# A linear-attention and long-convolution kernel with a new written-out order, the last inverse transform folded, and four output buffers

## The chip, the cores and the metric

The kernel runs on one core of a Trainium2 chip. The metric is the device time of one launch in microseconds: the median of three runs, and beside it one execution taken by the hardware profiler. The engines are named as the profile names them: PE (TensorE), DVE (VectorE), ACT (ScalarE), POOL (GpSimd), and SP, whose queue issues nearly all transfers.

## The reference, cut to what matters

Two layers, one behind the other, for 4 batches of 768 steps, 8 heads of 48 (together 384 channels):

```python
# 1: a recurrence over the steps, for each batch and head; state is 48 x 48
for t in range(S):
    cur   = einsum('bhd,bhe->bhde', u[None] * kt, vt)         # the "bonus"
    y[t]  = einsum('bhd,bhde->bhe', rt, state + cur)
    state = wt[..., None] * state + einsum('bhd,bhe->bhde', kt, vt)
# 2: x = y as (4, 768, 384)
x1, x2, x3 = split(x @ w_proj)                                # 384 -> 3 x 384
conv = irfft(rfft(x2, axis=1) * rfft(filter_fft, axis=0), axis=1)
out  = (x1 * conv * x3) @ w_out
```

## The kernel before, in words

**Chunks.** The steps are cut into chunks of 128, six to a batch, 24 in all; the number behind an operation's name is the chunk (`kq23`). Loads come in groups: chunks 0, 1, then 2 and 3, 4 and 5, and so on in pairs. For a chunk, `lw`, `lk`, `lr`, `lv` are its four loads of 192 KB (SP, L1313). `ln` takes the logarithm of w (ACT), `cs` sums it along the chunk (PE), `ex` takes the exponential in PSUM (ACT, L1353), `kq` multiplies it with k and r (DVE, L1356), `tr` and `qk` transpose that, `sc` is the product of scores in PSUM, `mt` copies it out under the causal mask: on DVE the mask is multiplied in (L1396), on ACT it is a plain copy and POOL cuts it afterwards (`mc`, L1401); either takes one half (letters D, A, G) or both halves at once (M, N, C). `kv`, `ki` and `su` carry the state on; `yi`, `ys`, `y` make the chunk's output in PSUM, `xn` copies it (or adds the bonus term on the way, letter V), `xa` adds the bonus on POOL after a copy to f32 (letter X), `yt` and `xT` transpose it for the second layer. The bonus term is `rk` (r times k), `ru` (the bonus product, times u), `rh` (halves added), `cc` (summed), `vc` (times v).

**Batches.** Names with two or three numbers belong to the second layer, the first number being the batch. `p` and `q` are the projections x1 and x3 (PE), `cp` copies x1 out, `cq` multiplies x3 in PSUM with it: the gate (DVE, L1649). `xw` and `cxw` make x2, `sd` adds and subtracts its two halves of the sequence, `f` is the forward transform as a matrix product, `cf` its copy, `u0`, `u1` and `p` followed by the batch and one more number (`p3.2`) the complex product with the filter's spectrum (DVE, L1695 to L1698), `E` the inverse transform for one block of 128 channels. Its copy `cE` (ACT) and two instructions `aE` on DVE (L1738, L1742) put the even and the odd part together. Where the inverse is folded (letter Q) PE multiplies fewer columns, 2 of 384 and 4 of 192 rather than 6 of 384, and `aE` leaves two interleaved halves in a second buffer, which the pair `dE` (L1751) adds and subtracts. `yE` multiplies with the gate, `o` is the last projection, `co` copies it out of PSUM to an output buffer, `so` stores that (SP, L1796). Batch 3 does this in smaller pieces: `sd`, `u` and `p` in thirds, `E3` in three parts for each block (`E3.2`, `E3.2.0`, `E3.2.2`), `o` in parts by block.

**Order.** Nothing is scheduled when the kernel runs. `ORDER` (L43 to L1068) lists all operations; each line has the name, the engine's letter, for PE the first PSUM bank, and at times the name of a DVE operation behind which this one is to start (a tie that keeps POOL and DVE apart, L1848). A `-` leaves an optional operation out. Each engine takes its operations strictly in that order and waits by semaphores. `warm n b` puts n filler matmuls on PE. Buffers are rings: three for w, four for k and r and for v, three for `xn`, and `NO` = 5 for the output; the ring's places are given in the order in which the stores are defined (batch 0: 0, 1, 2; batch 1: 3, 4, 0; batch 2: 1, 2, 3; batch 3: 4, 0, 1, 2). The last inverse, `E3`, is not folded; its six products `yE3` are on DVE but for `yE3.0.1` and `yE3.1.1`, which are POOL's.

Of the kernel before, what the change touches and what calls it, by code (L numbers as in the profile page):

```python
# [38 lines left out]
NLW, NLD, NG, NF, NS, NX, NO = 3, 4, 3, 4, 3, 3, 5  # L39
# [6 lines left out]
pads D  # L46
smalls D
zeros D
lw0 S
first A  # L50
ln0 A
imaps G
maske G smalls
maps G smalls
ang2 D
ang1 D
lw3 S
lw2 S
lr0 S
lk0 S  # L60
kz2 G
maskn G
cs0 P 4
kz0 G
ln2 A
u S
signs D
maski G
ia1.0 G
ex0 A  # L70
kq0 D
ia2.0 D
warm 9 1
cs3 P 6
kz3 G zeros
cs2 P 2
ur A
warm 5 1
um P 0
rk0 G  # L80
ub A
lv0 S
lw1 S
lr3 S
lk1 S
tr0 P 1
qk0 D
ph0 A
vb0 A
ex3 A  # L90
ln1 A
ang0 D
ru0 G ia2.0
rh0 G kq0
cc0 D
kz1 D
vc0 D
warm 6 0
sc0 P 0
warm 2 4  # L100
cs1 P 4
mt0.1 -
mt0.0 N
kv0 P 0
ex2 A
ex1 A
ia0.0 G zeros
su0 D
mc0.0 C cc0
lk3 S  # L110
lr1 S
mc0.1 -
warm 4 1
yi0 P 0
kq3 D
y0 P
xn0 A
tr3 P 1
kq1 D
lk2 S  # L120
lr2 S
lv1 S
lw4 S
lw5 S
tr1 P 0
rk1 G
ru1 D
rh1 G ru1
ph1 A
qk3 D  # L130
xa0 -
ph3 A
kq2 D
lv2 S
lv3 S
yt0 P 6
sc3 P 4
xT0 A
mt3.0 M
qk1 A  # L140
vb1 A
ph2 A
warm 4 7
tr2 P 6
lr4 S
lk4 S
ki1 P 1
sc1 P 2
qk2 A
mc3.0 -  # L150
mt1.1 -
kv1 P
warm 2 7
sc2 P 6
cc1 D
rk2 G
lk5 S
ru2 D
ia2.1 G
vc1 G  # L160
mc1.1 -
mt1.0 M
mc1.0 -
mt2.1 -
mt3.1 -
lr5 S
ln3 A
warm 5 0
cs4 P 4
yi1 P 2  # L170
rh2 G ru2
su1 D
vb2 G ru2
ys1 P
mc2.1 -
lv5 S
lv4 S
cc2 D
vc2 G cc2
mt2.0 M  # L180
wproj1 G mt2.0
ki2 P 0
y1 P
lw6 S
warm 5 1
kv2 P
xn1 A
ex4 A
cs5 P 2
xa1 -  # L190
mc2.0 -
yt1 P 1
su2 D
ki3 P 0
kv3 P
yi2 P 6
ys2 P
y2 P
mc3.1 -
xT1 A  # L200
kq4 D
# [259 lines left out]
ex11 A
p1.2.0 P 0
# [1416 lines left out]
```

## Time and profile before

| | |
|---|---|
| median of three runs | 157.35 us (157.31 to 157.82) |
| the profiled execution | 153.79 us, span 152.1 us |
| granted clock of TensorE | 1.0 throughout |
| busy: PE, DVE, ACT, POOL | 94%, 89%, 81%, 63% of the span |
| DMA | 26.23 MB; the last load issued at 108.2 us |

The profiled execution is 3.6 us shorter than the median of the runs; all times by stage are from the profiled one. Its rows give an instruction's mean duration in ns, or its start and duration in us; consecutive instructions of DVE overlap a little, so the busy time of a stretch is less than the sum of durations. `kq5` starts at 24.32 us, `kq7` at 35.55, `kq23` at 112.30 (it ends at 113.24); `p3.2`, DVE's last sum ahead of the last inverse, ends at 140.80, and DVE's last `yE3` at 146.17.

### The profile page before, as it was taken

How to read it: one execution, taken by the hardware profiler on the slowest of the kernel's cores; microseconds unless marked ns; L12 is line 12 of the kernel's file. 1: busy time of each engine (PE TensorE's matmuls, PEld its weight loads, DVE VectorE, ACT ScalarE, POOL GpSimd, SP SyncE). 2: the span in 40 equal slices, each digit the busy share in tenths (PEclk: the TensorE clock that was granted, in tenths of full speed). 3: DMA queues.
4: the chain of work that ended last, by engine and by line, in shares of the span. 5: the costliest groups of instructions: out<-in, count | busy, mean ns of one | idle time of the engine just before them, and what ended most of it. 6: DMA issues, size and time to landing. Idle time of an engine off the chain costs nothing.

```text
span 152.1 us, 4409 instructions
## 1 busy us (share of the span) xinstructions
PE 142.4 (94%) x1725; PEld 95.3 (63%) x1725; DVE 135.6 (89%) x252; ACT 123.1 (81%) x204; POOL 96.1 (63%) x101
## 2 busy tenths in 40 slices
PE   7986999999999999999999999999999999999980
PEld 5654667666556657567666776576687666656530
DVE  3589996989969999999989999999999999999950
ACT  4576849989979989997889899979999987576370
POOL 6577989944069567888968974885299164830310
PEclk9999999999999999999999999999999999999999
DMA  4999899999999999989899899998940000002956
GB/s 97 216 214 223 163 221 174 203 182 272 250 209 170 197 172 219 212 162 218 170 203 218 160 203 192 198 213 169 324 133 0 4 0 0 4 0 88 395 210 240
DMA packets 104118, 26.23 MB, mean 172 GB/s; under 512 B 100129, under 2 KB 102690, under 8 KB 104098
## 3 DMA queue, kind: packets, MB, share of 16 engines
q1 hardware_dynamic: 102498, 24.78, 74.2%
q0 software_dynamic: 1600, 1.18, 5.6%
q8 instruction: 13, 0.21, 0.5%
q14 instruction: 7, 0.06, 0.1%
HBM read 22.41 MB, written 4.72 MB: 178 GB/s over the span
## 4 chain that ended last, share of the span: by engine, by line
PE 42%; DVE 15%; DMA 13%; SPq 10%; ACT 8%; issue 5%; POOL 4%; POOLq 1%; DVEq 0%; ACTq 0%
SPq L1313 10%; PE banks L1624 7%; PE banks L1511 6%; PE banks L1780 5%; DMA w<-in_w_dram 5%; PE banks L1661 3%; PE banks L1368 3%; PE banks L1380 3%; DMA v<-in_v_dram 3%; DMA kr<-in_r_dram 3%; DVE kq L1356 3%; PE banks L1458 3%; DMA kr<-in_k_dram 2%; ACT banks L1353 2%; PE banks L1716 2%
## 5 line engine op out<-in xcount | busy, mean ns | idle before, releaser
L1209 POOL TENSOR_TENSOR rk<-kr 128x768 bf16<-128x768 f32 (+1 forms) x13 | 23.0, 1766 | 9.5 <-DMA kr<-in_r_dram 5.9
L1624 PE MATMUL banks<-xT,wproj 128*128 128x384 bf16 x144 | 27.9, 326 | 0.2 <-ACT x L1213 0.2
L1356 DVE TENSOR_TENSOR kq<-banks,kr 128x768 bf16<-128x768 f32 x24 | 22.4, 949 | 3.6 <-DMA kr<-in_k_dram 1.7
L1401 POOL TENSOR_SCALAR_AFFINE_SELECT mt<-mt 128x512 bf16<-128x512 bf16 (+1 forms) x15 | 14.0, 940 | 12.7 <-ACT mt L1213 8.6
L1209 POOL TENSOR_TENSOR vc<-vb,cc 128x768 bf16<-128x768 bf16 (+1 forms) x11 | 17.4, 1577 | 5.1 <-DVE cc L1332 3.3
L1353 ACT ACTIVATE banks<-banks 128x768 f32<-128x768 f32 x24 | 19.1, 806 | 0.5 <-PE banks L1350 0.2
L1624 PEld LDWEIGHTS <-wproj 128*128 128x128 bf16 x144 | 13.0, 97 | 8.1 <-issue 0.7
L1213 ACT ACTIVATE x<-banks 128x768 bf16<-128x768 f32 (+1 forms) x24 | 16.8, 709 | 1.6 <-PE banks L1661 1.1
L1396 DVE TENSOR_TENSOR mt<-banks,mask_excl 128x1024 bf16<-128x1024 f32 (+1 forms) x17 | 16.2, 965 | 0.2 <-PE banks L1380 0.2
L1213 ACT ACTIVATE qk<-banks 128x1024 bf16<-128x1024 bf16 x16 | 16.2, 1029 | 0.0
L1368 PE MATMUL banks<-ident,kq 128*128 128x128 bf16 x192 | 14.3, 219 | 1.4 <-ACT xn L1213 0.6
L1259 PE MATMUL banks<-wt 128*128 128x256 bf16 x90 | 14.4, 300 | 1.1 <-DVE wt L1282 1.1
L1368 PEld LDWEIGHTS <-kq 128*128 128x128 bf16 x192 | 11.8, 97 | 4.2 <-DVE kq L1356 1.6
L1780 PE MATMUL banks<-wout,y 128*128 128x384 bf16 x72 | 13.3, 326 | 0.5 <-DVE g L1649 0.3
L1661 PE MATMUL banks<-wproj,xT 128*128 128x384 bf16 x72 | 13.6, 325 | 0.0
L1511 PE MATMUL banks<-sd,F 128*128 128x384 bf16 (+1 forms) x96 | 13.4, 328 | 0.2 <-ACT phi L1360 0.2
L1319 ACT ACTIVATE lg<-w 128x768 bf16<-128x768 f32 (+1 forms) x13 | 10.4, 799 | 3.4 <-DMA w<-in_w_dram 3.4
L1213 ACT ACTIVATE mt<-banks 128x512 bf16<-128x512 f32 (+1 forms) x15 | 11.6, 802 | 1.1 <-PE banks L1380 0.7
L1213 ACT ACTIVATE o<-banks 128x768 f32<-128x768 f32 (+1 forms) x12 | 9.3, 785 | 3.5 <-PE banks L1780 3.4
L1511 PEld LDWEIGHTS <-F 128*128 128x128 bf16 (+1 forms) x120 | 8.5, 103 | 5.8 <-issue 1.1
L1649 DVE TENSOR_TENSOR g<-banks,x 128x384 bf16<-128x384 f32 (+1 forms) x16 | 11.8, 748 | 0.3 <-PE banks L1624 0.2
L1209 DVE TENSOR_TENSOR U<-X,hh 128x2304 bf16<-128x2304 bf16 (+1 forms) x12 | 11.9, 1022 | 0.0
(109 smaller groups left out, 331.1 us busy)
## 6 DMA issues: line engine op xcount, KB each, us to landing
w<-in_w_dram SPq DMA_DIRECT2D x24, 192.0 KB, 4.4
kr<-in_r_dram SPq DMA_DIRECT2D x24, 192.0 KB, 3.9
kr<-in_k_dram SPq DMA_DIRECT2D x24, 192.0 KB, 3.8
v<-in_v_dram SPq DMA_DIRECT2D x24, 192.0 KB, 3.9
out_dram<-o SPq DMA_DIRECT2D x11, 384.0 KB, 4.0
U<-in_moe_filter_fft_dram SPq DMA_DIRECT2D x1, 1152.0 KB, 7.3
wproj<-in_moe_w_proj_dram POOLq DMA_DIRECT2D x3, 288.0 KB, 5.9
out_dram<-o SPq DMA_DIRECT2D x2, 192.0 KB, 2.2
```

Of the source, the lines that this page charges most:

```text
L1209: return eng(e).tensor_mul(o, a, b)
L1213: return nc.scalar.activation(out=o, in_=a, func=AF.Copy)
L1259: nc.tensor.matmul(banks[:, at, 0:256], wt[:, 0:L], wt, start=True, stop=True)
L1313: op(f"l{name}{i}", [SP], lambda e, bk, t=t, x=x, q=q, rw=rw: nc.sync.dma_start(out=t[:, q], in_=x[b, :, rw, :].rearrange("h t d -> t h d" ...
L1353: op(f"ex{i}", [ACT], lambda e, bk: nc.scalar.activation(out=two(bk, f"cs{i}")[:, :, 0:C], in_=two(bk, f"cs{i}")[:, :, 0:C], func=AF.Exp), ...
L1356: op(f"kq{i}", [DVE], lambda e, bk: nc.vector.tensor_mul(kq[f][:, :, :, 0:D], two(bk, f"cs{i}")[:, :, 0:C].rearrange("p a (h d) -> p a h d ...
L1368: nc.tensor.transpose(p[:, HP * m + j, :], kq[f][:, m, 2 * j:2 * j + 2, :], ident)
L1396: return copy(ACT, o, x) if e in (ACT, ACT2) else nc.vector.tensor_mul(o, x, _mid(mask_excl, z - HP * a))
L1511: nc.tensor.matmul(p[rows], F[:, ti, c0 + rows.start:c0 + rows.stop], x[q][:, ti, :], start=(ti == 0), stop=(ti == NT - 1),)
L1624: nc.tensor.matmul(p, wproj[:, cb, col0:col0 + L], xT[bx][:, cb, sl], start=(cb == 0), stop=(cb == CB - 1),)
L1661: nc.tensor.matmul(view(bk)[:, z], xT[bx][:, cb, (c0 + z) * L:(c0 + z + 1) * L], wproj[:, cb, C:2 * C], start=(cb == 0), stop=(cb == CB - 1),)
L1780: nc.tensor.matmul(view(bk)[:, z], yt_[:, z, :], wout[:, cb, :], start=(cb == 0), stop=(cb == CB - 1),)
```

## The change

The order is written anew. It keeps the first layer's loops, the loads and the matrix products; what is moved is the place of nearly every operation in the first 30 us, of fewer behind that, and on which engine the movable ones run. `NO` goes from 5 to 4, so the ring's places are now 0, 1, 2 (batch 0), 3, 0, 1 (batch 1), 2, 3, 0 (batch 2), 1, 2, 3, 0 (batch 3). `xf`, the f32 buffer of the X way, goes from three places to one.

Four optional ways are added to the code. Of these the new order uses: the last inverse folded (all three blocks, with `dE3.2.1` and `dE3.0.1` on POOL and the other four `dE3` on DVE, and all six `yE3` on DVE), and the gate by way of an f32 buffer `xe` for `q0.2.1` and `q3.0.1` (`xq`, a copy on ACT; `gq`, the product on POOL). It doesn't use: the exponential to `xe` with the product on POOL (`ew`, `kw`) and `aE` on POOL (`aw`); all of these are listed with `-`. The bonus product's figure for DVE stands in no file of the kernel; nine of thirteen `ru` are on DVE before and after (`ru0` for `ru9`).

DVE's list ends so (before, after):

```diff
-p3.1 D   -p3.0 D   -p3.2 D   -cq3.2.1 D   -cq3.0.1 D
-aE3.0.1 D   -aE3.0.0 D   -aE3.1.1 D   -aE3.1.0 D   -aE3.2.0 D   -aE3.2.1 D
-yE3.2.1 D   -yE3.2.0 D   -yE3.0.0 D   -yE3.1.0 D   -co3.1 D
+yE2.0 D   +p3.1 D   +u03.2 D   +u13.2 D   +p3.0 D   +p3.2 D   +cq3.2.1 D   +cq3.2.0 D
+aE3.2.0 D   +aE3.2.1 D   +aE3.0.1 D   +aE3.0.0 D   +aE3.1.0 D   +aE3.1.1 D
+dE3.1.1 D   +yE3.0.1 D   +yE3.1.1 D   +yE3.2.1 D
+dE3.0.0 D   +dE3.1.0 D   +yE3.0.0 D   +dE3.2.0 D   +yE3.1.0 D   +yE3.2.0 D
```

POOL's, ACT's and SP's:

```diff
-rk12 G sd2.1.0   -mc20.0 G cq2.0.1   -vc11 G   -xa19 G   -dE1.2.1 G cc11   -dE1.0.1 G
-dE1.0.0 G aE1.1.0   -mc22.0 G yE1.1   -mc22.1 G   -mc23.0 C   -sd3.0.0 G sd3.1.0
-sd3.1.1 G   -sd3.1.2 G sd3.0.2   -dE2.0.0 G aE2.0.1   -dE2.1.1 G   -yE3.0.1 G aE3.0.0   -yE3.1.1 G
+mc20.0 G   +vc11 G   +rk12 G kq22   +dE1.0.1 G aE1.2.0   +xa18 G   +dE1.2.1 G   +rh12 G yE1.1
+mc22.0 C   +sd3.0.1 G sd3.1.2   +sd3.1.1 G sd3.1.2   +dE2.0.1 G   +dE2.0.0 G
+gq3.0.1 G p3.2   +dE3.2.1 G   +dE3.0.1 G aE3.0.0
...
-co2.0 A   -co2.1 A   -cE3.0 A   -cE3.1 A   -cE3.2 A   -co2.2 A   -co3.2 A   -co3.3 A   -co3.0 A
+xq3.0.1 X   +cf3.2 A   +cp3.2.1 A   +co2.2 A   +cE3.2 A   +cE3.0 A   +cE3.1 A   +co2.1 A   +co2.0 A
+co3.3 A   +co3.2 A   +co3.0 A   +co3.1 A
...
-lr23 S   -so0.1 S   -lk23 S   -so0.0 S   -so0.2 S   -lv22 S   -so2.0 S   -so1.1 S   -so1.2 S
-so1.0 S   -so2.1 S   -so2.2 S   -so3.2 S   -so3.3 S   -so3.0 S   -so3.1 S
+lr23 S   +lk23 S   +lk22 S   +so0.0 S   +lr22 S   +lv23 S   +so1.1 S   +so0.1 S   +so1.2 S
+so1.0 S   +so2.2 S   +so0.2 S   +so2.1 S   +so2.0 S   +so3.3 S   +so3.2 S   +so3.0 S   +so3.1 S
```

Further back, DVE loses and gains these (before `-`, after `+`):

```
 to kq5:         -ang2 -mt1.0:M -qk3 -kz1   +ur +ang2 (behind kq4) +qk1 +qk2 +ru0 +rh0 +rh2 +kz3 +ia1.0
 kq5 to kq7:     -cp0.2.0 -cxw0.0 -rh3 -xn3   +if0 +if1 +if3 +mt4.0 +mt4.1 +xT4 +xn2
 kq7 to kq23:    -cq0.2.1 -mt8.0:M -qk13 -qk15 -mt15.0 -mt15.1 -xT13 -cp2.2.1 -mt19.0:M -rh9 -rh10 -ru9
                 +mt8.0 +mt8.1 +xT10 +mt15.0:M +rh8 +xn14:V +yE0.1 +mt19.0 +qk18 +xT16 +xT17 +xn19:V
 kq23 to p3.2:   -rh12 -cq3.2.0 -sd3.0.1 -dE2.0.1   +dE1.0.0 +mt23.0:M +sd3.0.0 +sd3.1.2 +dE2.1.1
```

In the head SP's loads begin `lw0 lw3 lw2 lk0 lr0 u lk1 lr1 lw1 lr3 lk3 lv0` (before: `lw0 lw3 lw2 lr0 lk0 u lv0 lw1 lr3 lk1 lk3 lr1`), the copy `ur` moves from ACT to DVE ahead of `kq0`, and the fillers on PE go from 90 to 98. On PE behind the head the order is nearly the same; `yi18` goes out.

The code:

```diff
-NLW, NLD, NG, NF, NS, NX, NO = 3, 4, 3, 4, 3, 3, 5
+NLW, NLD, NG, NF, NS, NX, NO = 3, 4, 3, 4, 3, 3, 4
+NE = 2
...
+    xe = tiles(NE, [L, 2, H, D], FP32, "xe")
...
-    xf = sb.tile([L, NX, C], FP32, name="xf")
+    xf = sb.tile([L, 1, C], FP32, name="xf")
...
+            op("x" + n3, [WIDE, NONE], lambda e, bk: copy(ACT, x3, view(bk, n3)), w=["x" + n3], uses=[n3], cost=n)
+            op("g" + n3, [POOL, NONE], lambda e, bk: nc.gpsimd.tensor_mul(g[bx][:, fs, sl], x3, x1[:, fs, sl]),
...
-                    op(n if m == 1 else f"{n}.{m}", [PE], part(m, m == 1, m == 2),
+                    op(n if m == 1 else f"{n}.{m}", [PE, FOLD], part(m, m == 1, m == 2),
...
+            half = vl[cb].rearrange("p q h d -> p (q h d)").bitcast(BF16)[:, 0:S].rearrange("p (a t) -> p a t", a=2)
+
+            def other(bk):
+                return half if last else y2[1 - bx][cb]
...
-            if not last:
-                for z in (0, 1):
-                    op(f"d{n}.{z}", [DVE, POOL, NONE], lambda e, bk, z=z: eng(e).tensor_tensor(
-                        out=y[cb][:, z], in0=y2[1 - bx][cb][:, 0], in1=y2[1 - bx][cb][:, 1],
+            for z in (0, 1):
+                op(f"d{n}.{z}", [DVE, POOL, NONE], lambda e, bk, z=z: eng(e).tensor_tensor(
+                    out=y[cb][:, z], in0=other(bk)[:, 0], in1=other(bk)[:, 1],
...
```

## The prediction

> **What bounds the kernel now.** I read the page's busy sums and DMA row first, then a table of stretches, then VectorE's waits, then the groups by shape, and last the order of time around two places.
>
> ```profile
> PE 142.4 (94%) x1725; PEld 95.3 (63%) x1725; DVE 135.6 (89%) x252; ACT 123.1 (81%) x204; POOL 96.1 (63%) x101
> DMA  4999899999999999989899899998940000002956
> ```
>
> ```profile
> 24.30:60.00 35.70, 35.01 (x449) 23.29 (x446) 33.14 (x52) 32.76 (x50) 22.22 (x18) 1.00 1.04 204
> 60.00:113.20 53.20, 52.43 (x704) 35.94 (x702) 51.76 (x85) 48.44 (x84) 39.78 (x34) 1.00 0.98 202
> 113.20:146.20 33.00, 32.81 (x318) 20.76 (x316) 32.71 (x65) 24.37 (x41) 15.31 (x15) 1.00 0.16 61
> ```
>
> In the stretches the columns are PE, weight load, DVE, ACT, POOL. Between 24.3 us (the start of `kq5`) and 146.2 us (the end of the last product on the outputs) DVE is idle for 2.56 + 1.44 + 0.29 = 4.3 us of 121.9. PE looks as full, but its ends are modelled; `mt`, `qk`, `xn` and all else that it needs comes from DVE or ACT. The last loads land at about 114 us, so the 38 us behind them have no transfer to wait for.
>
> ```profile
> DVE kq L1356 <- DMA kr<-in_r_dram: 1.3, 1, 1.3
> DVE hh L1586 <- ACT hh L1585: 0.9, 1, 0.9
> ```
>
> These are the longest waits of DVE in that time; all others are 0.5 us or less. So from 24.3 us on, the end is set by the sum of DVE's work, and I make the sum of that.
>
> ```profile
> L1356 DVE TENSOR_TENSOR kq<-banks,kr 128x768 bf16<-128x768 f32 x24 | 22.4, 949 | 3.6 <-DMA kr<-in_k_dram 1.7 <-DMA kr<-in_r_dram 1.3 <-ACT banks L1353 0.4
> L1396 DVE TENSOR_TENSOR mt<-banks,mask_excl 128x1024 bf16<-128x1024 f32 x9 | 10.9, 1216 | 0.2 <-PE banks L1380 0.2
> L1396 DVE TENSOR_TENSOR mt<-banks,mask_excl 128x512 bf16<-128x512 f32 x8 | 5.3, 682 | 0.0
> L1751 POOL TENSOR_TENSOR y<-y 128x384 bf16<-128x384 bf16 x5 | 4.8, 986 | 0.5 <-DVE y L1738 0.4
> L1751 DVE TENSOR_TENSOR y<-y 128x384 bf16<-128x384 bf16 x7 | 2.1, 352 | 0.0
> ```
>
> ```profile
> 91.46 1.82 DVE L1356 TENSOR_TENSOR kq<-banks,kr 128x768 bf16<-128x768 f32 x2
> ...
> 122.92 2.24 DVE L1209 TENSOR_TENSOR U<-X,hh 128x2304 bf16<-128x2304 bf16 x1
> 120.97 2.99 POOL L1401 TENSOR_SCALAR_AFFINE_SELECT mt<-mt 128x512 bf16<-128x512 bf16 x3 [3.31 <-DVE y L1209]
> ```
>
> Two `kq` of 949 ns take 1.82 us together, so each instruction on a full DVE costs its duration less 0.08 us. The last two lines show the other cost: `u02.0` takes 2.24 us, the other five of its kind 1.34 (9.0 less 2.24, by 5); POOL's masks end at 123.96, and 1.20 us later it is done. It stood behind POOL.
>
> **The change, part by part (DVE, from `kq5` on).**
>
> Head (to `kq5`). `lv0` goes from sixth load to eleventh; by the landings of those places (8.3 and 12.7 us) `vb0`, `kv0` and then `su0` (12.3 us now) move to about 14.5, and DVE queues `vc0`, `cc1` and `kq2` behind `su0`. `ur` (0.5 us on ACT) now stands ahead of `kq0`; `ang2`, two `qk` and `ru0`, `rh0`, `rh2` come in, `mt1.0`, `qk3`, `kz1` go out. DVE is idle for 24.3 − 17.4 = 6.9 us here, and `kq5` waits for the last of the same 23 or 24 loads in both orders (24.2 us). I take 0, with 1 us against it if that cover is short. SP's loads otherwise change places within a few; two of the three stores among the last ones move behind them (about 1 us each: `so0.0` lands at 111.2, `so0.2` at 112.1), but `kq22` then waits for the load next to last, as `kq23` does now: 0. The eight more fillers on PE stand in front of waits: 0, at most 8 × 0.13 = 1 us (six took 0.76 in the chain), under the same cover.
>
> `kq5` to `kq7`. In: `mt4.0`, `mt4.1` (2 × 0.682), `xT4` (0.349), three flips. The trace has no flip on DVE; `dE` (0.352, both operands in SBUF) and the scaled copy `hg` from PSUM (0.552) bound it, and `dE` is nearer: 3 × 0.35. Out: `cxw0.0` (0.949), `cp0.2.0` (0.553), `rh3` (0.364). That is +0.90 for three more instructions: +0.65 us.
>
> `kq7` to `kq23`. In: `mt8` in two halves for one whole (+0.15), `xT10`, `xT16`, `xT17` (1.05), `xn14`, `xn19` (1.10), `yE0.1` (0.55), `rh8` (0.36), `qk18` (0.68). Out: `cq0.2.1` (0.55), `qk13`, `qk15` (1.37), `mt15` halves to a whole (0.15), `xT13` (0.35), `cp2.2.1` (0.55), one half of `mt19` (0.53), `rh9`, `rh10` (0.73), `ru9` (0.63). Sum −0.97 us with as many instructions. The copies and masks that go to ACT fall on an engine idle for 4.8 us of 53 there.
>
> `kq23` to `p3.2`. In: `mt23` (1.216, now on ACT), `dE1.0.0` and `dE2.1.1` (0.35 each), two pieces of `sd3` (0.43 each). Out: `rh12` (0.36), `dE2.0.1` (0.35), one `sd3` (0.43), and `cq3.2.0` (0.55) moves behind `p3.2`. +1.08, one more: +1.0 us.
>
> `p3.2` to the last `yE3`. The last inverse is folded: four `dE3` come to DVE (1.41), two `yE3` come from POOL (0.71), `cq3.2.0` comes here (0.55); `cq3.0.1` goes (0.95) to an ACT copy (0.81) and a POOL product. +1.72, six more: +1.23 us. The POOL product has no row; 0.91 (the 128x384 sum `xn<-xf,vc`) and 1.9 (the 128x768 f32 `rk`) bound it, and `rk` is nearer in size. It starts behind `p3.2`, the first `dE3` on POOL can start 2.2 us later, so it is hidden.
> A folded inverse's six matmuls take 0.66 us in the chain, six of 384 columns 0.97, so PE saves 3 × 0.31 = 0.9 us in E3, but DVE gets little of it: today E3's first copy ends 1.2 us behind `p3.2` and two gates (1.33) hide that; the gates that are left take 0.95, so 0.2 us opens.
>
> The end. Today 5.9 us lie between the last `yE3` on DVE (146.17) and the end:
>
> ```profile
> 143.23 0.85 POOL y L1209
> 144.15 0.95 POOLq L1874
> 145.15 1.16 PE banks L1780 x6
> 146.44 0.81 ACT o L1213
> 147.26 0.59 issue
> 147.85 0.56 DVE o L1215
> ```
>
> PE stands behind POOL's two products until 145.15. With them on DVE, after the last `yE3`: matmuls 0.6, `co3.0` 0.8, `co3.1` on ACT 0.4, then as now 3.7 from the last copy to the end: 5.5. −0.4 us.
>
> Four output buffers. `co1.1` to `co3.1` now wait for another store. The stores of batch 1 are long out; `so0.2`, now behind `so2.2` on SP, lands about 4 us behind `p3.2`, when ACT comes to `co2.0`. `so2.1` and `so2.0` are issued about 4 and 5 us behind `p3.2`; with the 2.3 us of a late store (145.35 to 147.69) they land at 6.3 and 7.4; `co3.2` and `co3.1` want their buffers at 6.5 and 8.3. I take 0; with today's longest late store (4.3) each would be 1 to 2 us late. Below zero: nothing, a buffer less frees nothing sooner.
>
> Clashes with POOL. `u02.0` loses 0.9 us now; the `mc23` it met is gone, since `mt23` masks on DVE. `ru9` (1.22 against 0.55) leaves DVE. New: `dE3.1.1` meets POOL's `dE3.0.1` (0.3), `dE1.2.0` meets `dE1.2.1` (0.3), and what I can't see in a new order, 0 to 2.4 (as much as now). Net I take −0.5, ends −1.5 and +1.5.
> The Trainium skill, page SBUF — State Buffer, section Who interferes with whom, has VectorE with two SBUF inputs and a GpSimd instruction that reads SBUF exclude each other, whichever starts first; by that rule every `dE`, `yE`, `u`, `p`, `ru` on DVE is exposed and `aE`, `kq`, `cq` (one operand in PSUM) aren't. The trace agrees: `u02.0` above ended 1.2 us behind POOL, and the two `kq` beside POOL's `rk10` kept 949 ns.
>
> Sum: 0 + 0.65 − 0.97 + 1.0 + 1.23 + 0.2 − 0.4 − 0.5 = +1.2; a little of the 4.3 us of idle time will close, −0.2. I forecast +1.0 us: the profiled execution from 153.8 (span 152.1) to 154.8; it lies 3.6 us below the median of the runs, 157.35, to which I add the same: 158.3.
>
> **The rivals.**
> Faster: the stalls close. For it: 4.3 us idle and 2.4 us of clashes on DVE between 24.3 and 146.2 us, which another order needn't have. Against it: six of the ten rows of DVE's waits there are 0.4 us or less. The sum without idle and clashes is +1.7 (the terms above less −0.5); it turns when more than 1.7 us of the 6.7 is won. Both large clashes (1.5) and half of the idle time (2) gone: 157.35 + 1.7 − 3.5 = 155.6.
> No change: DVE is not the pace. For it: the chain that ended last is 42% PE, and PE is as full; PE's own work falls by 1.2 us (E3; the `yi` of chunk 18, 0.26). Then DVE's 1.7 us and PE's saving about cancel: 157.3.
> Stores: `co3.2` and `co3.1` wait for `so2.1` and `so2.0`, 1 us on top: 159.3. For it: four late stores took 3 to 4.3 us when issued together; against it: single ones took 1.9 to 2.6.
> Clashes grow: three meetings of 0.67 to 0.9 more, 2 us on top: 160.3. For it: six `dE` and two `yE` with both operands in SBUF come into the last 30 us on DVE; against it: POOL's work after `rk12` falls by 2.9 us.
>
> **How the numbers follow.** Forecast 0.42, stalls close 0.30, no change 0.13, stores 0.08, clashes 0.07. About 0.3%, 0.47 us, is what a measurement of this kernel can tell from no change; so slower 0.57, same 0.13, faster 0.30. The forecast's own range is 157.9 to 159.3. The range of all reaches down to the middle of the faster case, 155.5, and up to 160.0: about 0.14 is left out below and 0.05 above.
>
> **What would show it.** Right: DVE again over 98% busy from `kq5` to the last `yE3`; `kq5` at 24 to 25 us, `kq23` starting at 111 to 113 (112.3 now); from its end to `p3.2`'s 27.5 to 28.5 us (27.6 now); from there 6.5 to 7 to the last `yE3` (5.4 now) and 5.5 to the end. Wrong: DVE with several us of idle time in the tail (then E3's folding put PE, ACT or a store in its place), `kq23` before 110.5 (stalls closed), `u`, `dE` or `yE` rows with means 0.1 us or more above today's (clashes), or ACT's copies `co3.*` waiting for a store.

## The result and the profile after

The changed kernel takes 157.91 us in the median of 20 executions (156.70 to 159.66); the kernel before, 156.73 us (154.53 to 157.82, 20 executions), so the medians differ by 1.2 us. The ratio is 1.0143 with an interval of 1.011 to 1.0176, some 2.2 us: slower either way, by less than 2%. The profiled execution took 157.75 us with a span of 156.0, against 153.79 and 152.1. That 153.79 is less than any of the 20 executions of the kernel before, so the two profiles lie further apart (3.9 us) than the kernels do. The ratios here leave out executions more than 1.5% above the fastest of their kernel (10 of the 20 of the kernel before, 4 of the changed kernel's); because the granted clock of PE will turn out to be a part of what happens, I also give medians of all executions and their clock.

The profile's page of the changed kernel: busy sums, the granted clock in 40 slices of 3.9 us, and the chain of work that ended last, by engine.

```profile
PE 144.9 (93%) x1731; PEld 97.2 (62%) x1731; DVE 139.3 (89%) x266; ACT 122.7 (79%) x203; POOL 93.3 (60%) x99
PEclk9999986789999999999999999999999999999999
PE 73%; DVE 9%; SPq 6%; POOL 3%; DMA 3%; issue 2%; ACT 1%; ACTq 0%; DVEq 0%; POOLq 0%
```

Three things differ from the page before. DVE is busy for 139.3 us rather than 135.6. The clock row, which was 9 in every slice, has a dip to 6 between 23 and 35 us. And the chain that ended last is PE's work for 73% (42% before) and DVE's for 9% (15%).

The table of stretches of the changed kernel, with the cuts of before moved along (start of `kq5`; 64.3 for 60.0, since the operations there are 4.3 us later; the end of `kq23`; the last `yE3`). Columns: PE, weight load, DVE, ACT, POOL, the clock, the DMA share and rate.

```profile
28.20:64.30 36.10, 34.93 (x420) 23.25 (x421) 33.17 (x56) 30.54 (x47) 18.12 (x13) 0.95 0.99 198
64.30:116.50 52.20, 52.05 (x700) 35.98 (x699) 50.50 (x85) 49.47 (x86) 41.92 (x35) 1.00 0.92 182
116.50:150.70 34.20, 32.83 (x324) 20.52 (x321) 33.84 (x72) 24.65 (x41) 12.94 (x13) 1.00 0.24 93
```

From `kq5` to the last `yE3` DVE does 117.5 us of work, as before (117.6), in 122.5 us rather than 121.9. So the stretch for which I made the sum has hardly moved. What moved is its beginning:

| | before | after | difference |
|---|---|---|---|
| start of `kq5` | 24.32 | 28.21 | +3.89 |
| `kq5` to `kq7` | 11.23 | 11.90 | +0.67 |
| `kq7` to `kq23` (starts) | 76.75 | 75.47 | −1.28 |
| `kq23` (start) to end of `p3.2` | 28.50 | 28.49 | 0 |
| `p3.2` to end of the last `yE3` | 5.37 | 6.63 | +1.26 |
| last `yE3` to the end | 5.91 | 5.30 | −0.61 |
| span | 152.08 | 156.00 | +3.92 |

The lines below the first add up to +0.04 us: the whole difference of the two profiles is made before `kq5`, in the term that I had put at nothing.

The prediction took DVE for the engine that sets the time behind `kq5`. The stretch from `kq7` to the end of `p3.2`, after and then before, with the same columns, shows something else:

```profile
40.11:144.07 103.96, 103.66 (x1280) 69.33 (x1278) 99.91 (x172) 91.04 (x154) 64.57 (x53) 1.00 0.73 150
```

```profile
35.55:140.80 105.25, 104.14 (x1283) 69.51 (x1282) 102.05 (x170) 92.72 (x157) 68.07 (x55) 1.00 0.75 156
```

PE is idle there for 0.3 us (1.1 before), DVE for 4.0 (3.2). DVE's work fell by 2.1 us and the stretch by only 1.3. It is 104.0 us long in six of the seven profiles taken of the changed order with the folded inverse, whatever happened ahead of it, and its last part, from `kq23` on, is 28.5 us in all thirteen profiles, with PE idle for less than 0.1 us. So by the profile it is PE that sets the time in these 104 us. This is read from traces in which the ends of PE's products are modelled; no run takes work from PE there, so it isn't tested.

Ahead of `kq5`, in order of time, DVE and then POOL in the changed kernel (start, us, what):

```profile
23.68 0.95 DVE L1322 TENSOR_TENSOR kq<-banks,kr 128x768 bf16<-128x768 f32 x1
24.54 3.19 DVE L1616 TENSOR_SCALAR o<-o,tcol 128x384 int32<-128x384 f32 x1
27.66 0.41 DVE L1619 TENSOR_SCALAR o<-o,tcol 128x384 int32<-128x384 f32 x1
28.10 0.15 DVE L1620 TENSOR_SCALAR o<-tcol 128x1 int32<-128x1 f32 x1
28.21 0.96 DVE L1322 TENSOR_TENSOR kq<-banks,kr 128x768 bf16<-128x768 f32 x1
```

```profile
23.44 1.48 POOL L1322 TENSOR_TENSOR vc<-vb,cc 128x768 bf16<-128x768 bf16 x1
24.86 0.80 POOL L1409 DMA_DIRECT2D wproj<-in_moe_w_proj_dram  x1
25.69 1.82 POOL L1322 TENSOR_TENSOR rk<-kr 128x768 bf16<-128x768 f32 x1
```

The three L16xx lines are `ang2`, between `kq4` and `kq5`. It had taken 0.98 us at 3.65 us in the order before. Here its first instruction is 3.19 us long while its twin on the next line, of the same shape, is 0.41; it ends 0.2 us after POOL's `rk3`. `kq4`, which reads a bank of PSUM, is 0.95 us long, as ever, beside POOL's `vc2`.

The windows of the same stretch, after and then before:

```profile
20.00:24.00 4.00, 3.13 (x44) 2.06 (x41) 3.38 (x5) 2.29 (x4) 3.97 (x5) 0.81 1.05 209
24.00:28.00 4.00, 3.39 (x63) 2.74 (x61) 4.00 (x3) 2.39 (x4) 3.49 (x3) 0.76 1.16 196
28.00:32.00 4.00, 2.77 (x31) 2.13 (x32) 3.28 (x8) 2.77 (x5) 0.20 (x1) 0.67 1.09 191
32.00:36.00 4.00, 4.00 (x42) 2.51 (x42) 3.87 (x9) 3.98 (x6) 2.94 (x3) 0.91 0.89 166
```

```profile
24.00:28.00 4.00, 3.86 (x68) 2.65 (x66) 3.59 (x8) 3.80 (x6) 3.75 (x4) 1.00 1.15 164
28.00:32.00 4.00, 3.79 (x49) 2.57 (x47) 3.92 (x6) 3.86 (x5) 3.91 (x5) 1.00 1.04 190
```

Here PE is idle for 0.6 to 1.2 us of each of the first three windows, and its granted clock is below 1 in all four; before, it was idle for 0.14 and 0.21 us of the two windows shown and had 1.00.

Last, waits of DVE (from 28.2 us on), of PE (between 18 and 24 us) and of ACT (from 140 us on), and the chain at the very end.

```profile
DVE hh L1706 <- ACT hh L1705: 1.1, 1, 1.1
DVE mt L1516 <- PE banks L1500: 0.7, 1, 0.7
...
PE banks L1561 <- POOL vc L1322: 0.9, 1, 0.9
...
ACT o L1326 <- DMA out_dram<-o: 0.4, 1, 0.4
```

```profile
147.92 0.36 DVE y L1894
148.28 0.28 DVE y L1322
148.56 0.05 issue
148.61 2.72 PE banks L1924 x15
```

DVE's long waits behind `kq5` are of the size they had. One copy to an output buffer waits 0.4 us for a store (`co2.0` for a store that landed at 147.45), and ACT is then idle for 1.5 us before `co3.3`, so that wait costs nothing. At the end PE no longer stands behind POOL: it is the first `dE3` and the first `yE3` on DVE that release it.

### The profile page after: what moved, and what is told of

Its sections match the earlier page's. It is cut to its first block, busy times and chain, and to the rows that moved or that the text cites. A ratio compares the mean times of both kernels' runs of the same rounds, so it can differ in the third digit from the quotient of the medians.

```text
span 156.0 us, 4430 instructions
## 1 busy us (share of the span) xinstructions
PE 144.9 (93%) x1731; PEld 97.2 (62%) x1731; DVE 139.3 (89%) x266; ACT 122.7 (79%) x203; POOL 93.3 (60%) x99
## 4 chain that ended last, share of the span: by engine, by line
PE 73%; DVE 9%; SPq 6%; POOL 3%; DMA 3%; issue 2%; ACT 1%; ACTq 0%; DVEq 0%; POOLq 0%
PE banks L1744 15%; PE banks L1631 9%; PE banks L1785 8%; PE banks L1924 6%; PE banks L1488 6%; SPq L1426 6%; PE banks L1841 5%; PE banks L1500 4%; PE banks L1578 4%; DMA kr<-in_k_dram 3%; PE banks L1602 3%; PE banks L1541 2%; DVE o L1616 2%; PE banks L1460 2%; PE banks L1570 2%; DVE kq L1322 2%
## 5 line engine op out<-in xcount | busy, mean ns | idle before, releaser
L1521 POOL TENSOR_SCALAR_AFFINE_SELECT mt<-mt 128x512 bf16<-128x512 bf16 (+1 forms) x16 | 13.2, 831 | 11.8 <-ACT mt L1326 11.6
L1326 ACT ACTIVATE x<-banks 128x768 bf16<-128x768 f32 (+1 forms) x27 | 18.5, 694 | 1.8 <-PE banks L1744 0.8
L1516 DVE TENSOR_TENSOR mt<-banks,mask_excl 128x512 bf16<-128x512 f32 (+1 forms) x19 | 16.9, 906 | 0.7 <-PE banks L1500 0.7
L1488 PE MATMUL banks<-ident,kq 128*128 128x128 bf16 x192 | 15.2, 225 | 2.5 <-DVE kq L1322 2.4
L1372 PE MATMUL banks<-wt 128*128 128x256 bf16 x98 | 15.7, 300 | 1.1 <-DVE wt L1395 1.1
L1488 PEld LDWEIGHTS <-kq 128*128 128x128 bf16 x192 | 12.5, 101 | 5.4 <-DVE kq L1322 3.9
L1442 POOL TENSOR_TENSOR rk<-rk 128x384 bf16<-128x384 bf16 (+1 forms) x8 | 8.2, 1030 | 9.9 <-DVE rk L1322 9.8
L1326 ACT ACTIVATE o<-banks 128x768 f32<-128x768 f32 (+1 forms) x13 | 9.8, 760 | 5.5 <-PE banks L1924 4.2
L1785 PE MATMUL banks<-wproj,xT 128*128 128x384 bf16 x72 | 13.9, 333 | 0.0
L1372 PEld LDWEIGHTS <-wt 128*128 128x128 bf16 x98 | 9.3, 107 | 3.2 <-DVE wt L1395 1.1
```

The lines of the kernel that those rows point to most:

```text
L1326: return nc.scalar.activation(out=o, in_=a, func=AF.Copy)
L1372: nc.tensor.matmul(banks[:, at, 0:256], wt[:, 0:L], wt, start=True, stop=True)
L1488: nc.tensor.transpose(p[:, HP * m + j, :], kq[f][:, m, 2 * j:2 * j + 2, :], ident)
L1516: return copy(ACT, o, x) if e in (ACT, ACT2) else nc.vector.tensor_mul(o, x, _mid(mask_excl, z - HP * a))
L1521: return nc.gpsimd.affine_select(out=o, in_=o, pattern=[[0, z - HP * a], [1, L]], compare_op=ALU.is_gt, fill=0.0, base=0, channel_multipli ...
L1785: nc.tensor.matmul(view(bk)[:, z], xT[bx][:, cb, (c0 + z) * L:(c0 + z + 1) * L], wproj[:, cb, C:2 * C], start=(cb == 0), stop=(cb == CB - 1),)
```

## The experiments

The question is the 3.9 us ahead of `kq5`. Theory one: DVE stands behind POOL at `ang2`, 2.7 us. Theory two: PE's clock falls there, and each fall slows all that follows until it is back. Rival: the difference lies in the end after all (the folded inverse), or in something that the profiled execution has only by chance. In the table, "before" is the kernel before on the same chip at the same time, and the last column counts the executions in which PE's mean granted clock was 0.993 or more, that is, in which it fell, as far as the profiles show, at most in the last 2 us or so (the profiles of `a_fill` and `b_nofill`, at 0.994 and 0.993, have their only fall in the last 1.8 and 2.2 us of the span). The expectations count from 0.995.

| run | median, all executions | before | ratio, interval | clock ≥ 0.993 |
|---|---|---|---|---|
| the changed kernel, first 20 | 157.91 | 156.73 | 1.0143, 1.011 to 1.0176 | 3 of 20 |
| `b_again` (before, unchanged) | 154.30 | 154.18 | 1.0004, 0.9962 to 1.0046 | 8 of 10 |
| `a_again` (changed kernel, unchanged) | 157.37 | 154.53 | 1.0097, 1.0004 to 1.019 | 1 of 11 |
| `a_ang2_early` | 155.68 | 154.18 | none | 2 of 6 |
| `b_ang2_late` | 154.45 | 154.18 | 0.9979, 0.9939 to 1.0019 | 7 of 13 |
| `a_unfold` | 155.63 | 154.18 | 1.0080, 1.0035 to 1.0125 | 4 of 12 |
| `a_fill` | 155.12 | 154.53 | 1.0027, 0.9979 to 1.0075 | 8 of 11 |
| `a_fill_early` | 155.81 | 154.53 | 1.0055, 1.0008 to 1.0102 | 11 of 11 |
| `b_nofill` | 154.61 | 154.53 | 0.9989, 0.9944 to 1.0034 | 8 of 11 |
| `c_pool_waits` | 155.18 | 154.73 | 1.0014, 0.9963 to 1.0065 | 5 of 10 |
| `c_ia_late` (one execution) | 156.25 | 154.73 | none | 0 of 1 |
| `c_all` | 156.35 | 154.73 | none | 2 of 4 |

Of the kernel before, 57 of the 74 executions beside these runs (other than the first 20, whose clock isn't on record) had a clock of 0.993 or more. Beside these runs the kernel before is 2.0 to 2.5 us faster than in its first 20 executions and the changed kernel (`a_again`) only 0.5 us, so that it lies 2.8 us above and not 1.2.

### Moving `ang2` alone, both ways, and both kernels again

```diff
 # a_ang2_early: the changed kernel's list
 ang1 D
+ang2 D
...
 kq4 D
...
-ang2 D
 # b_ang2_late: the list before
-ang2 D
...
 kq4 D
...
+ang2 D
```

> The changed kernel with one move: ang2 stands right behind ang1, where DVE waits 1.2 us for the load of u, and no longer between kq4 and kq5. Collision theory: the 3.7 us that ang2 took (24.5 to 28.2 us) are 1.0 of work and 2.7 of standing behind vc2, wproj0 and rk3 on POOL; kq5 then starts at 24.6 to 25.5 instead of 28.2 and the time falls by 2.5 to 3.5 us, to 0.99 of the kernel before or a little under. Load theory (the head is late because lv0 and lk2 land later and POOL makes ia0.1 and ia1.1 ahead of vc1): ang2's stall only fills a wait that is there anyway, kq5 comes at 27 and the time falls by 1 us at most. Clock theory (PE ran at 0.67 to 0.81 of its clock from 20 to 32 us): the clock stays low and with it the time, within 0.5 us.

> The kernel before with the same move the other way: ang2 behind kq4. Collision theory: it meets wproj1, wproj0 and rk3 on POOL (22.7 to 26.3 us), ends at about 26.7 instead of taking 1.0 us, kq5 starts at 26.7 instead of 24.3, and the time rises by 2 to 2.5 us. Load theory and clock theory: kq5 waits for its load until 24.2 us anyway, ang2 fills that wait, no change (within 0.4 us).

> The kernel before, unchanged, for a second profile of it: its profiled execution was 2.9 us under the median of its 20 runs, the changed kernel's only 0.2 us. If the head of the kernel before varies from run to run, this profile shows kq5 or kq7 1 to 3 us later than 24.3 and 35.6 us, with the rest as it was; if the runs differ by their ends or the clock, kq5 is at 24 to 25 us again.

In its early place `ang2` takes 0.93 us again in the changed kernel, `kq5` starts at 25.35 us (28.21 with it late) and its profile's span is 155.1 rather than 156.0. It doesn't gain the 2.9 us that `kq5` gained: `kq5` to `kq7` is now 13.9 us instead of 11.9, with the clock at 0.5 from 21.7 to 28.6 us. In the median, 155.68 us, it is 1.5 us above the kernel beside it, where the expectation had it a little under. The page's clock row, and DVE's wait for PE in that stretch:

```profile
PEclk9999985899999999999999999999999999999999
```

```profile
DVE xn L1328 <- PE banks L1578: 2.0, 1, 2.0
```

In the late place in the kernel before, it shows the same thing as in the changed one, at the other instruction of its pair. DVE, then POOL:

```profile
24.00 2.78 DVE L1499 TENSOR_SCALAR o<-o,tcol 128x384 int32<-128x384 f32 x1
```

```profile
22.93 1.79 POOL L1296 DMA_DIRECT2D wproj<-in_moe_w_proj_dram  x2
24.74 1.82 POOL L1209 TENSOR_TENSOR rk<-kr 128x768 bf16<-128x768 f32 x1
```

`ang2` takes 3.55 us, `kq5` starts at 27.00, the clock falls to 0.5 from 27.3 to 34.2 us, and the span is 155.6. So one moved operation makes both signs of the changed kernel appear in the kernel before. Yet the median of the runs, expected to rise by 2 to 2.5 us, stays (154.45 against 154.18); the executions spread instead, from 152.65 to 157.34 us, the three with a clock below 0.98 at 156.2 to 157.3 and seven with 0.993 or more at a median of 153.5. Theory one is therefore shown for the profiles, and is not the whole of the time: the place of `ang2` alone doesn't make the kernel slow each time. `b_again` gives the same as the kernel beside it and puts its own scatter at 152.9 to 157.7 us; its profile has `kq5` at 24.26 us.

### The inverse unfolded

```diff
-E3.2 Q 0   -E3.0 Q 2   -E3.1 Q 4        (and their parts)
+E3.2 P 0   +E3.0 P 2   +E3.1 P 4
-dE3.2.1 G   -dE3.0.1 G   -dE3.1.1 D   -dE3.0.0 D   -dE3.1.0 D   -dE3.2.0 D
+dE3.2.1 -   +dE3.0.1 -   +dE3.1.1 -   +dE3.0.0 -   +dE3.1.0 -   +dE3.2.0 -
```

> The changed kernel with the last inverse not folded: E3 as six products of 384 columns for each block, no dE3; yE3 stay on DVE. By the prediction's tail: DVE loses four dE3 (1.1 us) and a clash of 0.3; PE's 0.9 us more stand beside DVE's work; the stretch from p3.2 to the last yE3 falls from 6.6 to 5.2 to 5.6 us and the time by 1.0 to 1.4 us (0.7 to 0.9%). Rival: folding paid for itself because PE holds the copies cE3 up: the stretch stays at 6.3 to 6.8 us and the time within 0.4 us.

`p3.2` to the last `yE3` is 5.70 us (6.63 folded), but from there to the end it is 6.11 (5.30). Together 11.81 against 11.93: all but 0.1 us of what DVE wins is given back. From the end of the first `yE3` to the end of the span both kernels take 7.45 us: behind it the chain runs over PE's products of the last projection, one after another, and not over the `dE3` and `yE3` that are still to come on DVE. So the fold is no explanation of the slowdown; unfolded, the kernel is still 0.8% above the kernel before. In the same profile the clock stayed at 1.0 and POOL happened to pause at the right moment. POOL, then DVE:

```profile
22.11 1.47 POOL L1322 TENSOR_TENSOR vc<-vb,cc 128x768 bf16<-128x768 bf16 x1 [0.18 <-ACT banks L1469]
23.53 0.80 POOL L1409 DMA_DIRECT2D wproj<-in_moe_w_proj_dram  x1
25.73 1.80 POOL L1322 TENSOR_TENSOR rk<-kr 128x768 bf16<-128x768 f32 x1 [1.40 <-DMA kr<-in_k_dram]
```

```profile
23.77 0.72 DVE L1616 TENSOR_SCALAR o<-o,tcol 128x384 int32<-128x384 f32 x1
24.41 0.40 DVE L1619 TENSOR_SCALAR o<-o,tcol 128x384 int32<-128x384 f32 x1
```

`rk3` waits 1.40 us for its load; DVE's instruction ends 0.16 us behind `wproj0` and the rest of `ang2` gets through, 1.23 us in all. In the changed kernel's own profile POOL paused for only 0.03 us between `wproj0` and `rk3`, and DVE was not let in. How long `ang2` takes thus hangs on when a transfer lands.

### Fillers for the clock

```diff
 # a_fill: 15 more filler matmuls in front of three waits; a_fill_early has ang2 early as well
-warm 2 4      (ahead of sc2)
+warm 6 4
-warm 3 7      (ahead of yi1)
+warm 10 7
-warm 2 5      (ahead of tr4)
+warm 6 5
 # b_nofill: the kernel before without two groups of fillers, ahead of cs4 and kv2
-warm 5 0
-warm 5 1
```

> The changed kernel as it is, on the chip and in the rounds of these runs, and for a second profile: mean clock under 0.995 in most executions; those at 0.995 or more are 1 to 2.5 us faster than the others. ang2 takes 1 to 4 us from one profile to another, if its stall depends on whether POOL's vc2 has begun.

> The changed kernel with 15 more filler matmuls on PE, at three places between 18 and 25 us (in front of sc2 2 to 6, yi1 3 to 10, tr4 2 to 6). Clock theory: PE is idle often enough between 16 and 25 us that its granted clock falls to half for 3.4 to 6.8 us in most executions; with the fillers the mean clock is 0.995 or more in at least three quarters of them (as shipped, 2 of 20) and the time falls by 1.5 to 2.5 us. Collision theory (ang2 behind three POOL instructions): the clock may come back, but ang2 still stands, and the time falls by less than 1 us. If fillers only delay PE, it rises by up to 1 us.

> Both at once: those 15 fillers, and ang2 right behind ang1. If clock and collision both cost, kq5 starts at 24.6 to 25.7 us, kq7 at 36 to 37, the clock is 0.995 or more in most executions, and the time is 2.5 to 3.5 us under the changed kernel's, 0 to 1 us above the kernel before (what is left is the tail's 1.2 us less some in the middle). If only the clock costs, it is no better than the fillers alone; if only the collision costs, no better than the early ang2 with a clock of 1.0 (155.6 us there in one execution, 153.2 in another).

> The kernel before without ten of its fillers (five in front of cs4, five in front of kv2, 18.9 to 21.3 us); nothing else. Clock theory: PE falls to half clock in that stretch in at least half of the executions (mean clock 0.97 to 0.99) and these take 1.5 to 3 us longer. If fillers hold nothing up: clock as before (0.995 or more in three quarters), time within 0.4 us.

The fillers do work that nobody reads, and the median falls from 157.37 to 155.12 us; 8 of 11 executions keep the clock where 1 of 11 did. (From 0.995 on, as the expectation counts, it is 6 of 11 and not three quarters; of the kernel before beside it, 18 of 33, and of the changed kernel's first 20, 3 and not 2.) The intervals of the two ratios overlap, and so do the executions, 153.68 to 158.36 and 154.61 to 159.04 us, so the gain of 2.25 us is likely rather than certain. What a fall goes with differs. The table has the medians of the executions by their clock, and how many there are:

| | 0.993 or more | 0.98 to 0.99 | below 0.98 |
|---|---|---|---|
| `a_again` | 154.61 (1) | 157.32 (6) | 158.49 (4) |
| the changed kernel, first 20 | 157.65 (3) | 157.89 (11) | 158.48 (6) |
| the kernel before, beside `a_again` | 154.29 (24) | 154.87 (6) | 157.27 (3) |

So a lower clock goes with a longer time in each row, but the 2.7 us of `a_again` rest on one execution; the other rows have 0.2 and 0.6 us for the first step. The fillers support theory two; what a fall costs stays open. Its reverse failed: without ten of its fillers the kernel before is unchanged (154.61 against 154.53, 8 of 11 at 0.993 or more, as 24 of 33 beside it), so those ten neither cost time nor keep the clock.

`ang2` early on top of the fillers gave nothing (155.81), although all eleven executions keep the clock and its profile has `kq5` at 24.32, where it was before: 0.8 us are lost again by `kq7` and another 0.7 to 2.4 by `kq23` (against the four profiles of the order before), in waits of DVE of up to 1.0 us each. With both causes out of the way the kernel is thus still 1.3 us above the kernel before in the median (0.85 by the ratio).

The fillers leave theory one as it was: in the profile of `a_fill` `ang2` takes 3.45 us, and a second operation meets the same fate 9 us later. DVE, then POOL:

```profile
35.62 1.89 DVE L1681 TENSOR_SCALAR mx<-mi,sgn 128x384 bf16<-128x384 bf16 x1
```

```profile
35.58 1.81 POOL L1322 TENSOR_TENSOR rk<-kr 128x768 bf16<-128x768 f32 x1 [2.48 <-DMA kr<-in_r_dram]
```

This is `if1`, one of the three flips that the change brings to DVE; it takes 0.31 us where POOL is idle. Here it begins 0.04 us after `rk4` and ends 0.12 us after it. The same flip took 0.96 in the changed kernel's profile and 1.47 in that of `a_ang2_early`, and `if3` 1.86 in that of `a_again`.

### POOL made to wait

```diff
-wproj0 G cc2
+wproj0 G ang2
...
-rk4 G
+rk4 G if1
```

> The changed kernel with two waits put in on POOL, and nothing moved: wproj0 (and so rk3 behind it) waits for ang2, and rk4 waits for if1. In the changed kernel's profile ang2 took 3.71 us behind POOL's vc2, wproj0 and rk3 in a row, and in three other profiles if1 or if3 (0.25 to 0.31 us where nothing is beside them) took 0.96 to 1.89 us with POOL's rk4 beside them. Theory A (DVE's f32 instructions out of SBUF stand still until POOL pauses): ang2 takes at most what is left of vc2 plus 0.93, 1.0 to 2.0 us; if1 and if3 take 0.25 to 0.35; kq5 starts 1.7 to 2.6 us after kq4 ends, against 3.6 now; rk3 and rk4 start later by 1 to 2 us and hold nothing up; 1.5 to 2.5 us off the changed kernel where the clock does the same in both, so about 155 to 156 us where the changed kernel has 157.4. Theory B (ang2 is long for a reason of its own, its input or its place behind kq4): ang2 3.4 us or more again, kq5 as late as before, time as the changed kernel. Theory C (what the waits free is only lost again because PE's clock still falls to 0.5 in this stage): ang2 short, and kq5 to kq7 13 us or more, with a granted clock below 0.99 in most runs and a median within 1 us of the changed kernel's.

Nothing is moved and no work is taken away. DVE, then POOL:

```profile
24.86 0.41 DVE L1616 TENSOR_SCALAR o<-o,tcol 128x384 int32<-128x384 f32 x1
25.18 0.41 DVE L1619 TENSOR_SCALAR o<-o,tcol 128x384 int32<-128x384 f32 x1
25.63 0.15 DVE L1620 TENSOR_SCALAR o<-tcol 128x1 int32<-128x1 f32 x1
25.74 0.96 DVE L1322 TENSOR_TENSOR kq<-banks,kr 128x768 bf16<-128x768 f32 x1
```

```profile
23.37 1.48 POOL L1322 TENSOR_TENSOR vc<-vb,cc 128x768 bf16<-128x768 bf16 x1
26.09 0.80 POOL L1409 DMA_DIRECT2D wproj<-in_moe_w_proj_dram  x1 [1.24 <-DVE o L1620]
26.92 1.82 POOL L1322 TENSOR_TENSOR rk<-kr 128x768 bf16<-128x768 f32 x1
```

`ang2` takes 0.93 us, both flips 0.25 and 0.31, `kq5` comes 0.8 us after `kq4` ends (1.7 to 2.6 expected), and the median is 155.18 us, 0.45 above the kernel before beside it (ratio 1.0014, 0.9963 to 1.0065). Theory one is right in what it says of the three operations, and the other theory, that `ang2` is long by itself, falls. The clock holds in 5 of 10 executions (1 of 11 in `a_again`); in the one shown it was 0.5 from 21.4 to 28.2 us, so that `kq5` to `kq7` took 12.7 us and `kq7` came only 1.7 us sooner than in the changed kernel. Theory C of the expectation is thus seen in that profile, but its median, within 1 us of the changed kernel's, is not.

### Two inverses behind `rk3`, and all together

```diff
 # c_ia_late (and in c_all)
-ia0.1 G   -ia1.1 G     (ahead of vc1)
 rk3 G
+ia1.1 G   +ia0.1 G
```

> The changed kernel with POOL's ia0.1 and ia1.1 moved from ahead of vc1 to behind rk3. Theory (kq4 is 1.6 us late because vc1 waits behind these two, 1.69 + 0.76 us, and PE's yi1 behind vc1): vc1 starts 2.2 to 2.5 us sooner after rk2's end (at once, against 2.4 us), PE's wait for vc at yi1 (0.9 us) is gone, and kq4 starts 0.8 to 1.6 us earlier against the landing of k's third load, at 22.1 to 23.0 where it had 23.0 to 24.0. Rival (PE itself, with its half clock, or ACT sets kq4): kq4 within 0.3 us of where it was relative to kq2. One look, by the stage and not by the whole time.

PE's wait of 0.9 us for `vc1` is gone, but `vc1` starts 1.6 us after `rk2`, not at once, since it waits for `rh2`. `kq4` is then not sooner: it stands behind its load. DVE's waits from 22 to 28 us:

```profile
DVE kq L1322 <- DMA kr<-in_k_dram: 2.8, 2, 1.8
```

`kq4` and `kq5` wait 2.8 us between them; the load `lk5`, issued at 20.1 us in this execution and 19.2 in the profile before, landed at 26.78, a late one (24.5 in three others of the changed order, 25.7 in `a_unfold`). Counted from `kq2`, `kq4` is 0.9 us later than in the changed kernel, so the rival fits no better than the theory; what the run settles is that in this execution a load and not the wait at `vc1` set `kq4`. The late load also holds `rk3` back, POOL is idle for 2.6 us ahead of it, and `ang2` takes 0.97 us.

> The changed kernel with all four at once: the 15 fillers added for PE's clock, the two waits on POOL, ia0.1 and ia1.1 behind rk3, and the last block's products left unfolded. If the causes add up as the runs so far have them (2.3 us by the fillers in the median, 1.5 to 2.5 by the waits on POOL, about 1 by the unfolded block, up to 1 by ia): kq5 at 24 to 25, kq7 at 35 to 36.5, last yE3 5.4 to 5.9 us after p3.2's end, span 150 to 152, 152 to 153.5 us, that is 0.5 to 1.5% below the kernel before on this chip (about 154.3). If they overlap (each takes away the same idle time): 154 to 155.5, no faster than the kernel before. If the clock still falls: above 155.5 with a granted clock below 0.99.

The causes don't add up: 154.47 to 156.90 us in four executions, no better than the kernel before. In its profile the clock is 1.0 and `ang2` takes 1.17 us, and a new wait has come:

```profile
DVE cc L1445 <- POOL rk L1442: 1.8, 1, 1.8
```

`cc3` waits for `rh3`, which POOL reaches late, because `wproj0` and `rk3` now start behind `ang2` and the two inverses stand behind them. `kq5` to `kq7` is 12.9 us. No version that I tried is faster than the kernel before.

## Why the prediction was right in the sum and wrong in a step

The forecast was 158.3 us, 1.0 above the kernel before; measured were 157.91 us, 1.2 above the kernel before beside it in the median, and 2.2 by the ratio. Step by step:

- **Head to `kq5`: 0, with 1 us against it. This is the step that failed.** It was +3.9 us in the profile. I let 6.9 us of DVE's idle time cover whatever came in. But that idle time is not where the new work is: of these 6.9 us 5.4 lie ahead of `kq2` and only 1.5 between `kq2` and `kq5`, where `ang2`, copies and `ru` were put. In that stretch DVE's busy time went from 7.11 to 10.83 us (2.7 of it the stall, 1.0 `ang2` itself), and the idle time ahead of `kq2` remained (5.4 us). I had also priced `ang2` at its duration in its old place, 0.98 us, where POOL has nothing beside it; behind `kq4` POOL works without a pause. I had counted clashes as a term for "what I can't see in a new order, 0 to 2.4", and listed the `dE`; `ang2` and the flips, which read SBUF alone as well, were not in my list of exposed instructions, and the new clash was there, 2.7 and 0.7 us. Of the 3.9 us, 2.3 lie between `kq4` and `kq5`; the rest is `kq4`, 1.6 us later. It starts at 23.68 to 23.99 us in the three profiles whose clock falls before it, at 22.36 to 23.26 in the six others of the changed order and at 22.08 to 22.56 in the four of the order before, so the clock has a part in that; the loads and the wait for `vc1` have others, which I can't separate.
- **PE's clock** was in no step. The only profile that I had showed 1.0 throughout, and I didn't ask how much idle time it could bear; "fillers 0" was right for their cost, and left out what they are for.
- **`lv0` later, 0:** `kv0` went from 11.7 to 13.9 and `su0` from 12.3 to 14.3 us as I had said, and `kq2` started 0.7 us later.
- **`kq5` to `kq7`, +0.65:** +0.67 in the pair of profiles, but not for my reason alone: 0.66 us of it is `if1` behind POOL and the clock is low at its beginning. In `a_unfold`, with neither, the stretch is 11.04 us, 0.2 less than before; the added work went into idle time, which fell from 1.0 to 0.5 us.
- **`kq7` to `kq23`, −0.97:** −1.28 in the pair of profiles, near it for another reason. DVE's work there fell by 2.0 us, not 0.97, and PE, idle for 1.1 us before and 0.3 after, sets the length. The four profiles of the order before have 75.65 to 77.44 us here, a spread larger than the term.
- **`kq23` to `p3.2`, +1.0, and the clash of `u02.0`, −0.9:** together 0.0. But PE is idle for 0.00 us of these 28.5 in both orders, so the length tells nothing of DVE's two terms. The clash itself did go: `u02.0` takes 1.35 us (2.24 before), with no mask of POOL's beside it:

```profile
127.29 1.35 DVE L1322 TENSOR_TENSOR U<-X,hh 128x2304 bf16<-128x2304 bf16 x1
```

- **`p3.2` to the last `yE3`, +1.23 and a bubble of 0.2:** +1.26, with DVE idle for less than 0.1 us at a time. The four `dE3` on DVE take 354 ns each, as taken from `dE`. The POOL product without a row, `gq3.0.1`, took 1.65 us (bounds 0.91 and 1.9) and was hidden: POOL's `dE3.2.1` starts 0.33 us behind it.

```profile
L1894 DVE TENSOR_TENSOR y<-v x4: 351/354/358, 147.9 to 149.8; 128x384 bf16<-128x384 bf16 x4
```

- **The end, −0.4:** −0.61.
- **Four output buffers, 0:** right; late stores took 2.3 us in the median, as assumed, and the one wait of 0.4 us is hidden. The rival of the stores is out. Five buffers with the rest of the change were not tried.
- **A little idle time closes, −0.2:** it grew, from 4.3 to 5.0 us between `kq5` and the last `yE3`, a little in each of the three stretches. DVE was busy for 95.9% of that time rather than "over 98%", which it hadn't been before either (96.5%).

By the profile my terms behind `kq5` come to +1.0 and measured +0.04. Over all profiles taken, `kq5` to the end is 127.9 us in the mean for the four of the order before and 128.8 for the seven with the changed order and the folded inverse, +0.8, with single ones from 126.9 to 130.6. That is not my reason either: 0.7 of it lies between `kq5` and `kq7`, where flips stand behind POOL and the clock is low, and behind `kq7` the two means differ by 0.1 us. So it was luck that the sum fell inside the range. For the profiled execution I had forecast 154.8 us, and it took 157.75. The forecast for the median came out because the medians lie closer together than the two profiles: the profiled execution of the kernel before was faster than all of its 20 others, and the median of three to which I added the change was 0.6 us above that of the 20.

The rival "no change" (0.13) had the pace of the 104 us behind `kq7` as the profile shows it, with PE, but not the time. The rival "clashes grow" (0.07) named the right mechanism with the wrong place and size: three meetings in the tail with 2 us in all. They came in the head, 2.7 and 0.7 us in the profile.

What stays open is how much of the slowdown is POOL and how much the clock. Taking away either (`c_pool_waits`, `a_fill`) brings 2.2 to 2.4 of the 2.8 us that `a_again` lies above the kernel beside it, so they are not two independent sums. The one can also lead to the other. The clock's falls have two places. In `b_ang2_late`, `a_again` and the second fall of the changed kernel they begin at 27.3 to 29.3 us, while PE waits 1.8 to 2.6 us for `kq5`, which stands behind `ang2` (in `c_ia_late` at 28.1 us, where `kq5` waits for its load). In `a_ang2_early`, `c_pool_waits` and the first fall of the changed kernel they begin at 21.4 to 22.5, ahead of `ang2`, after PE's waits around `vc1` (0.6, 0.3 and 0.9 us between 16.8 and 21.5 in the changed kernel).

Within one profile the clock changes on a fixed grid of 3.41 us, so the profiles can be cut into its windows. The two ahead of the falls of the changed kernel:

```profile
19.10:22.52 3.42, 2.20 (x38) 1.47 (x37) 3.39 (x6) 2.00 (x3) 3.33 (x6) 1.00 1.06 209
25.93:29.34 3.41, 1.58 (x43) 1.28 (x42) 3.38 (x5) 1.16 (x3) 1.58 (x1) 1.00 1.28 220
```

PE was busy for 2.20 and 1.58 us of them. In all thirteen profiles, up to 45 us, the four windows at full clock with less than 1.6 us of PE's work were each followed by a fall, of the ten with 1.8 to 2.26 us three were, and none with more. So the same wait of PE can bring a fall or not, as it lies to the grid: in the profile of `a_fill` PE waits 2.25 us behind `ang2`, but across the border of two windows, with 2.11 and 2.26 us of work, and the clock holds. The busy time isn't the whole rule, since near the end of `a_fill_early` and `c_all` windows with 1.48 and 1.56 us kept the clock.

## What to carry to other kernels

Idle time covers new work only if it lies behind the point where that work can start: cut an engine's idle time at each wait for a load, and count what is left behind the last one. Before moving an operation of DVE that works from SBUF to SBUF, read what POOL does at the new place: the price is not the instruction's duration but the time to POOL's next pause. A stretch in which PE already has little to spare for its clock needs several executions, since one profile can show it at full clock and the next at half. And before adding up one engine's work, see which engine is idle least in that stretch: here it was PE, and DVE's sum said little of the time.

## What the runs showed of the hardware

**A DVE instruction out of SBUF can stand behind several POOL instructions in a row.** `ang2`'s instruction of 0.41 us took 3.19 behind the rest of `vc2`, `wproj0` and `rk3`, with gaps of 0.03 us or less between them; a gap of 1.40 us let it through in `a_unfold`, and gaps made by a wait did so in `c_pool_waits`. It need not stand so long: in `a_fill` and `a_again` the same instruction came through 0.2 us behind the end of `vc2`, although `wproj0` followed at once, and only its twin then stood through `wproj0` and `rk3` (2.69 and 2.66 us). What decides between the two no run shows. A POOL instruction that only issues a transfer seems to hold it too (0.72 us beside `wproj0` in `a_unfold`, ending 0.16 us behind it). `kq4`, with one operand in PSUM, kept its 0.95 us beside `vc2`. The Trainium skill, page SBUF — State Buffer, section Who interferes with whom, has whoever issues first hold the shared ports for the whole instruction and the other block, and names `tensor_scalar` among those that can be concerned. The trace agrees as to who is blocked; what it shows beyond that is that the end of POOL's instruction doesn't always free DVE when the next one of POOL follows within 0.03 us.

**PE's granted clock is 1.0 or 0.5 and changes in steps of 3.41 us.** It was 0.5 for 22.52 to 25.93 and 29.34 to 32.76 us in the changed kernel, for 6.83 us in `a_ang2_early` (21.73 to 28.56), `b_ang2_late` (27.34 to 34.17) and `c_pool_waits` (21.38 to 28.21), for 3.41 us in `a_again` (28.69 to 32.10); the phase differs between executions of one kernel. The Trainium skill, page TensorE: Matmul & The Clock Gate, section Part 1: The HAM clock gate (the "warmup" mystery), tells of two states, half and full, and a free-running window of about 3.4 us after whose idle passing the clock drops; the trace agrees with both. But no window here was idle: by the profile PE was busy for 0.80 to 2.23 of the 3.41 us ahead of the seven falls before `kq7`. What one window at half clock costs the kernel isn't settled: the median at 0.98 to 0.99 lies 0.2, 0.6 and 2.7 us above that at 0.993 or more (first 20 executions of the changed kernel, kernel before beside `a_again`, `a_again`), the last against a single execution.
